# Chunk-selecting attention with a squared-ReLU layer behind it: the first three half-batches transposed on TensorE and placed from PSUM

## The chip, the cores and the metric

One core of a Trainium2 chip runs the whole program. The metric is the device time of one execution in microseconds (us). TensorE is called PE below, VectorE DVE, ScalarE ACT, GpSimd POOL and the SyncE queue SP, as in the rows of the profile.

## The reference

Four batches, eight heads, 768 positions, head width 64. The keys of a head are cut into 24 chunks of 32. For each query an upper bound of its score with each chunk is worked out from the chunk's smallest and largest key values, chunks that lie ahead of the query are ruled out, and the six best chunks are kept. Attention runs over the kept chunks under the causal mask, and a layer with a squared ReLU follows:

```
k_min, k_max = min and max of k over each chunk of 32
ub     = sum_d max(q * k_min, q * k_max)          # one bound per query and chunk
sel    = the 6 chunks with the largest ub, causal
scores = where(sel & causal, q k^T / 8, -1e9)
x      = softmax(scores) v                        # [3072, 512] over all heads
out    = relu(x w_in)^2 w_out                     # 512 -> 2048 -> 512
```

## The kernel before

**Slots.** A batch is cut into two halves of 384 queries (a *half-batch*, `hb` 0 to 7), and the eight heads into four pairs. One half-batch of one pair is a *slot*: `slots` (L171) counts 32 of them, four for each `hb`. The order of the work is written out by hand: nothing is reordered, each engine takes its instructions in program order, and waits are placed where one engine needs another's result.

**What a slot does.** `step_P` (L290) brings keys and queries of a pair into the transposed layout (width on partitions), takes minima and maxima of the key chunks (`extrema`, L184: two DVE reductions and a product into `kbd`) and the two ReLUs of the queries, `qr`. `step_U` (L298) multiplies them into the bounds `ub` on PE and finds the sixth largest with DVE's MAX8; the comparison is written beside the queries as a 0/1 row block. `step_V` (L320) transposes that block on PE and copies it out of PSUM into `qc`, so that one matmul of `kc` by `qc` in `step_E` (L347) gives score and penalty at once; ACT takes the exponential, and POOL cuts the diagonal blocks with an affine_select (L366). `step_F` (L374 to L395) multiplies by the values, and DVE divides (L391, L392). `kc` holds the keys in one half of the partitions and the chunk codes (`oneh`) in the other, and the two heads of a pair have them the other way round, so that one head's rows have to change partitions.

**Running ahead.** While slot s is in `step_E`, `step_U` and `step_V` are those of slot s+1, and `step_P` that of slot s+2.

**How keys and queries get there.** For `hb` 0 `stage` (L101) loads f32 by 16 DMAs on the SP and ACT queues; `step_cast` (L177) casts keys on DVE and queries on ACT, and `step_T0` (L195) transposes on PE into two PSUM tiles, `tk` for the keys and `tq` for the queries. For `hb` 1 `step_T1` (L250) transposes on PE, ACT copies both to SBUF (L260), and four small SP DMAs per slot (`place_k` L230, `place_q` L237) move them into `kc` and `qc`. From `hb` 2 on six DMA transposes per half-batch (`tr`, L265, on SP) write `kT` and `qT`, four larger SP DMAs place them, and `step_K` (L274) takes the extrema of all four pairs on DVE in two passes, for minima and maxima.

**The other work.** The layer behind the attention is cut into 16 `ffn_up` pieces (L432: four matmuls, ReLU on ACT or DVE, square on DVE) and 12 `ffn_down` pieces per half-batch, kept in `queue` and drawn by `fill` and `f1` between the attention steps. The ups of `hb` 0 run in the slots 4 to 8; the downs begin in slot 8. Loads from HBM other than the staged ones are casting DMAs on the POOL queue. `at(s, ...)` (L475) notes loads, chunk codes and DMA transposes for a slot, and `go` (L518) issues them there.

The PSUM pools are `psS` (three score tiles), `psF` (two, for `ph` and the transposes), `psY` (one, for the downs) and `psA` (two, tag `att`, for `ub`, `qt`, `po`, `pt`). Two lines set what the text below turns on, the DMA transposes of `hb` 2 and the place of the placing of slot 6, both on SP:

```
at(s0 + (i // 3 if hb > 2 else 0), tr, hb, "kq"[i // 3], i % 3)   # L514: all six of hb 2 in slot 4
(place_k if n == "k" else place_q)(1, p, p + 1)                   # L261: step_P(6) issues it at the end of slot 4
```

Of the kernel before, what the change touches and what calls it, by code (L numbers as in the profile page):

```python
# [14 lines left out]


CH = 32
TOPK = 6
HT = 3
# [5 lines left out]

# [4 lines left out]
)  # L30


@with_exitstack
def kernel(
# [30 lines left out]

    QROW = (D, 0)
    SROW = (0, D)
    kcs = [[consts.tile([128, NP, S], BF16, tag=f"kc{i}_{h}", name="kc") for h in range(2)]
           for i in range(2)]
    qcs = [consts.tile([128, NP, 2, HB], BF16, tag=f"qc{i}", name="qc") for i in range(2)]  # L70
# [3 lines left out]

# [13 lines left out]
    def load_v(b, h0, h1, j0, j1):  # L88
        if j1 - j0 == 1:
            nc.gpsimd.dma_start(  # L90
                out=vn[b % 2][:, h0:h1, j0, 0:D],
                in_=v[b, h0:h1, 128 * j0:128 * j1].rearrange("h p d -> p h d"))
        else:
            nc.gpsimd.dma_start(
                out=vn[b % 2][:, h0:h1, :, 0:D],
                in_=v[b, h0:h1].rearrange("h (j p) d -> p h j d", p=128))


    staged = []

    def stage(p, pool):  # L101
        t = []
        for eng, src in ((nc.sync, k), (nc.scalar if p < 2 else nc.sync, q)):
            x = pool.tile([128, HT, 2, D], F32, tag=f"st{len(t)}", bufs=NP, name="stage")
            for hh in range(2):
                eng.dma_start(
                    out=x[:, :, hh, :],
                    in_=src[0, 2 * p + hh, 0:HB].rearrange("(j p) d -> p j d", p=128))
            t.append(x)
        staged.append(t)  # L110

    ctx.enter_context(tc.manual_schedule())
    early = ExitStack()
    epool = early.enter_context(tc.tile_pool(name="early", bufs=NP))
    for p in range(NP):
        stage(p, epool)

    oneh = consts.tile([D, S], BF16, tag="oneh")
    nc.vector.memset(oneh, 0.0)
    cmask = consts.tile([128, HT, 2, NC], BF16, tag="cmask", name="cmask")  # L120
    nc.vector.memset(cmask, 0.0)
    ident = consts.tile([128, 128], BF16, tag="ident")
    make_identity(nc, ident)
    nc.gpsimd.affine_select(
        out=oneh, in_=oneh, compare_op=ALU.not_equal, fill=OFFSEL,
        base=0, channel_multiplier=1, pattern=[[-1, NC], [0, CH]])

    for g in range(4):
        nc.gpsimd.affine_select(
            out=cmask[g * 32:(g + 1) * 32], in_=cmask[g * 32:(g + 1) * 32],  # L130
            compare_op=ALU.is_ge, fill=NEG,
            base=12 + g, channel_multiplier=0,
            pattern=[[4, HT], [0, 2], [-1, NC]])
# [11 lines left out]
    for h in range(2):  # L145
        nc.vector.tensor_copy(
            kcs[0][h][SROW[h]:SROW[h] + D, :, 0:HB],
            oneh[:, 0:HB].unsqueeze(1).to_broadcast([D, NP, HB]))
# [3 lines left out]
    def codes(i, p, c0):  # L152
        for h in range(2):
            nc.vector.tensor_copy(kcs[i][h][SROW[h]:SROW[h] + D, p, c0:S], oneh[:, c0:S])

    def clear():
        nc.gpsimd.memset(vn[1][:, :, :, D:D + 1], 1.0)
        for i in range(3):
            nc.gpsimd.memset(nsel[i], 0.0)

# [13 lines left out]
    kbd = {}  # L174


    def step_cast(p):  # L177
        t = staged[p]
        kst = work.tile([128, HT, 2 * D], BF16, tag="kst", name="kst")
        nc.vector.tensor_copy(kst.rearrange("p j (h d) -> p j h d", h=2), t[0])  # L180
        nc.scalar.copy(qn0[:, :, p, 1:3, :], t[1])
        st[p] = {"kst": kst}

    def extrema(kt, s):  # L184

# [9 lines left out]
    def step_T0(s):  # L195

        p = s
        t = st[s]
        tk = psF.tile([128, HB], BF16, tag="ph", name="tk")
        tq = psF.tile([128, HB], BF16, tag="ph", name="tq")  # L200
        for j in range(HT):
            nc.tensor.matmul(tk[:, 128 * j:128 * (j + 1)], lhsT=t["kst"][:, j, :],
                             rhs=ident, is_transpose=True, start=True, stop=True)
        for j in range(HT):
            nc.tensor.matmul(tq[:, 128 * j:128 * (j + 1)],
                             lhsT=qn0[:, j, p, 1:3, :].rearrange("p h d -> p (h d)"),
                             rhs=ident, is_transpose=True, start=True, stop=True)
        qr = t["qr"] = work.tile([128, 2, HB], BF16, tag="qr", bufs=3, name="qr")
        nc.scalar.activation(qr[:, 0, :], tq, ACT.Relu, scale=-1.0)
        nc.scalar.activation(qr[:, 1, :], tq, ACT.Relu)  # L210
        extrema(tk, s)
        nc.vector.tensor_copy(kcs[0][0][D:128, p, 0:HB], tk[0:D])
        t["tk"] = tk

    def step_T0b(s):
        nc.scalar.copy(kcs[0][1][0:D, s, 0:HB], st[s]["tk"][D:128])
# [3 lines left out]
    def half_T(hb):  # L220
        if hb not in tT:
            tT[hb] = [work.tile([128, NP, HB], BF16, tag=f"{n}T", name=f"{n}T")
                      for n in "kq"]
        return tT[hb]

    def place_k(hb, p0, p1):
        kT = tT[hb][0]
        c = HB * (hb % 2)
        for h in range(2):
            nc.sync.dma_start(  # L230
                out=kcs[hb // 2 % 2][h][QROW[h]:QROW[h] + D, p0:p1, c:c + HB],
                in_=kT[D * h:D * h + D, p0:p1, :])

    def place_q(hb, p0, p1):
        qT = tT[hb][1]
        for h in range(2):
            nc.sync.dma_start(  # L237
                out=qcs[hb % 2][QROW[h]:QROW[h] + D, p0:p1, h, :],
                in_=qT[D * h:D * h + D, p0:p1, :])

    def relus(s):
        qT = tT[s // NP][1]
        t = st.setdefault(s, {})
        qr = t["qr"] = work.tile([128, 2, HB], BF16, tag="qr", bufs=3, name="qr")
        p = slots[s][2]
        nc.vector.tensor_scalar(qr[:, 0, :], qT[:, p, :], -1.0, 0.0,
                                op0=ALU.mult, op1=ALU.max)
        nc.vector.tensor_scalar_max(qr[:, 1, :], qT[:, p, :], 0.0)

    def step_T1(s):  # L250

        b, half, p = slots[s]
        for n, dst in zip("kq", half_T(1)):
            x = psF.tile([128, HB], BF16, tag="ph", name=f"t{n}")
            for j in range(HT):
                nc.tensor.matmul(
                    x[:, 128 * j:128 * (j + 1)],
                    lhsT=nat[n, b, HT + j][:, 128 * p:128 * (p + 1)],
                    rhs=ident, is_transpose=True, start=True, stop=True)
            nc.scalar.copy(dst[:, p, :], x)  # L260
            (place_k if n == "k" else place_q)(1, p, p + 1)  # L261
        extrema(tT[1][0][:, p, :], s)
        relus(s)

    def tr(hb, n, j):  # L265

        b, half = hb // 2, hb % 2
        nc.sync.dma_start_transpose(  # L268
            out=half_T(hb)["kq".index(n)][:, :, 128 * j:128 * (j + 1)],
            in_=nat.pop((n, b, HT * half + j)))  # L270

    kms = {}

    def step_K(hb, w):  # L274
# [3 lines left out]
        x = tT[hb][0].rearrange("p a (c j) -> p (a c) j", j=CH)  # L278
# [11 lines left out]
    def step_P(s):  # L290
        if s >= 2 * NP:
            relus(s)
        elif s >= NP:
            step_T1(s)
        else:
            step_T0(s)
# [353 lines left out]
```

## Time and profile before

| what | value |
|---|---|
| median of three runs | 306.75 us (306.55 to 307.5) |
| span of the profiled execution, first to last instruction | 305.8 us |
| that execution's own time | not listed apart from the runs; the median lies 0.95 us over the span |
| PE busy | 258.0 us (84%) |
| DVE, ACT busy | 174.4 us, 174.2 us (57% each) |
| POOL busy | 92.0 us (30%) |
| mean granted PE clock | 0.959 |

The page cuts the span into 40 slices of 7.6 us and writes the busy share of each engine in tenths. A row of the timeline has start, duration, engine, line, operation, output and inputs, and in brackets the idle time of the engine ahead of it with what ended it. A row of the waits has the waiting instruction, what it waited for, the sum, the number of times and the longest. A row of the windows has a stretch, its length, then busy time and instructions of PE, PE's weight load, DVE, ACT and POOL, the granted clock, the DMA share and GB/s.

### The profile page before, as it was taken

To read this page: it belongs to the slowest core of one execution; us is meant where nothing else is said; L and a number is where in the kernel's file an instruction comes from. 1 tells how busy PE (TensorE), PEld (TensorE's weight loads), DVE (VectorE), ACT (ScalarE), POOL (GpSimd) and SP (SyncE) were. 2 spreads that over 40 slices of the span, in tenths; PEclk is the share of its full clock that TensorE was granted. 3 is DMA by queue.
4 is the path that set the end of the run, shared out by engine and by line. 5 is a ranking of instruction groups with operands and counts; after the bars stand their busy time and mean duration, and the time that the engine had idled before them with its cause. 6 is when DMAs were issued, how large, how long until landed. Compare 5 with 4: busy or idle time off the path is not lost.

```text
span 305.8 us, 6296 instructions
## 1 busy us (share of the span) xinstructions
PE 258.0 (84%) x2260; PEld 157.7 (52%) x2260; DVE 174.4 (57%) x648; ACT 174.2 (57%) x372; POOL 92.0 (30%) x136
## 2 busy tenths in 40 slices
PE   2776682076589998999999989999999999999994
PEld 1554351054355655666556556665565666555541
DVE  6796684039777852775377537754775453332321
ACT  4584663036256684777666847776668677544300
POOL 8967441014434242353341423511112011000000
PEclk9999798579689999999999999999999999999999
DMA  9999999999957759799798398995442100010011
GB/s 159 158 187 111 176 124 179 157 162 146 130 41 59 146 81 146 72 177 166 95 143 160 66 147 85 168 143 102 89 139 71 51 12 26 34 38 34 35 70 69
DMA packets 117008, 33.32 MB, mean 109 GB/s; under 512 B 103664, under 2 KB 112880, under 8 KB 116976
## 3 DMA queue, kind: packets, MB, share of 16 engines
q0 software_dynamic: 71568, 12.85, 60.4%
q1 hardware_dynamic: 43808, 19.67, 31.4%
q10 hardware_dynamic: 1600, 0.39, 0.6%
q8 instruction: 18, 0.29, 0.5%
q14 instruction: 14, 0.11, 0.1%
HBM read 27.26 MB, written 6.29 MB: 110 GB/s over the span
## 4 chain that ended last, share of the span: by engine, by line
PE 64%; DMA 10%; SPq 9%; DVE 8%; ACT 5%; issue 2%; POOL 1%; POOLq 0%; DVEq 0%; ACTq 0%
PE py L454 24%; PE ph L435 21%; PE ps L357 9%; PE po L382 6%; SPq L268 6%; DMA qc<-qT 6%; DMA xT<-x 3%; SPq L419 2%; ACT e L362 2%; PE ub L307 1%; DVE kst L180 1%; ACT ht L442 1%; DVE km L282 1%; DMA stage<-in_k_dram 1%; ACT qc L344 1%
## 5 line engine op out<-in xcount | busy, mean ns | idle before, releaser
L362 ACT ACTIVATE e<-ps 128x512 bf16<-128x512 f32 x192 | 96.3, 549 | 40.1 <-PE ps L357 39.4
L435 PE MATMUL ph<-xT,w_in 128*128 128x384 bf16 x512 | 104.3, 331 | 7.3 <-ACT kT L260 3.3
L454 PE MATMUL py<-w_out,h 128*128 128x512 bf16 x384 | 96.6, 379 | 0.0
L444 DVE TENSOR_TENSOR h<-ht 128x384 bf16<-128x384 bf16 x128 | 47.8, 376 | 76.2 <-ACT ht L442 75.6
L442 ACT ACTIVATE ht<-ph 128x384 bf16<-128x384 f32 x120 | 58.9, 494 | 46.6 <-PE ph L435 44.7
L366 POOL TENSOR_SCALAR_AFFINE_SELECT e<-e 128x384 bf16<-128x384 bf16 x64 | 34.0, 532 | 167.6 <-ACT e L362 167.4
L357 PE MATMUL ps<-qc,kc 128*128 128x384 bf16 (+2 forms) x320 | 59.3, 291 | 16.0 <-DMA qc<-qT 14.3
L435 PEld LDWEIGHTS <-w_in 128*128 128x128 bf16 x512 | 47.7, 99 | 40.3 <-issue 8.5
L454 PEld LDWEIGHTS <-h 128*128 128x128 bf16 x384 | 35.8, 98 | 31.3
L357 PEld LDWEIGHTS <-kc 128*128 128x128 bf16 x320 | 28.1, 101 | 33.1 <-issue 17.2
L382 PEld LDWEIGHTS <-e 128*128 128x128 bf16 x672 | 27.3, 101 | 7.7 <-POOL e L366 2.7
L382 PE MATMUL po<-vn,e 128*128 128x65 bf16 x672 | 28.8, 198 | 2.1 <-POOL e L366 1.4
L314 DVE MAX8 m<-ub 128x8 f32<-128x24 f32 (+1 forms) x160 | 16.6, 169 | 6.3 <-PE ub L307 6.2
L83 POOL DMA_DIRECT2D qn<-in_q_dram x21 | 18.7, 901 | 0.1
L83 POOL DMA_DIRECT2D kn<-in_k_dram x21 | 18.6, 894 | 0.1
L392 DVE TENSOR_TENSOR x<-po,r 128x384 bf16<-128x384 f32 x32 | 17.8, 557 | 1.1
L460 ACT COPY ob<-py 128x512 f32<-128x512 f32 x18 | 10.7, 593 | 9.2 <-PE py L454 9.1
L282 DVE TENSOR_TENSOR km<-km 128x384 bf16<-128x384 bf16 (+3 forms) x48 | 13.8, 287 | 1.7
L338 PE MATMUL qt<-ident,nsel 128*128 128x128 bf16 x72 | 8.7, 222 | 6.4 <-DVE nsel L315 5.8
L440 DVE TENSOR_SCALAR ht<-ph 128x384 bf16<-128x384 f32 x8 | 4.4, 553 | 16.8 <-PE ph L435 16.6
L307 PE MATMUL ub<-kbd,qr 128*128 128x48 bf16 (+1 forms) x160 | 9.5, 180 | 4.9 <-DVE kbd L191 2.7
L343 DVE COPY qc<-qt 64x384 bf16<-64x384 bf16 (+1 forms) x28 | 8.9, 317 | 5.8 <-PE qt L338 5.8
(68 smaller groups left out, 166.5 us busy)
## 6 DMA issues: line engine op xcount, KB each, us to landing
out_dram<-ob SPq DMA_DIRECT2D x24, 256.0 KB, 2.2
kn<-in_k_dram POOLq DMA_DIRECT2D x21, 128.0 KB, 4.2
qn<-in_q_dram POOLq DMA_DIRECT2D x21, 128.0 KB, 5.3
vn<-in_v_dram POOLq DMA_DIRECT2D x6, 384.0 KB, 8.0
kc<-kT SPq DMA_DIRECT2D x12, 192.0 KB, 6.6
qc<-qT SPq DMA_DIRECT2D x12, 192.0 KB, 6.7
w_in<-in_moe_w_in_dram POOLq DMA_DIRECT2D x2, 1024.0 KB, 10.8
w_out<-in_moe_w_out_dram POOLq DMA_DIRECT2D x1, 2048.0 KB, 25.0
```

The source lines that it names most:

```text
L83: nc.gpsimd.dma_start(out=t.rearrange("p (h d) -> p h d", d=D), in_=(q if n == "q" else k)[b, :, 128 * j:128 * (j + 1)] .rearrange("h p d ...
L268: nc.sync.dma_start_transpose(out=half_T(hb)["kq".index(n)][:, :, 128 * j:128 * (j + 1)], in_=nat.pop((n, b, HT * half + j)))
L282: nc.vector.tensor_tensor(y, x[:, :, 0:m], x[:, :, m:2 * m], op=op)
L357: nc.tensor.matmul(ps[:, at:at + 128 * m], lhsT=kcs[b % 2][hh][:, p, 128 * j:128 * (j + 1)], rhs=qcs[half][:, p, hh, c:c + 128 * m], start ...
L362: nc.scalar.activation(e[:, 512 * n + lo:512 * n + hi], ps[:, lo:hi], ACT.Exp, scale=float(scale))
L366: nc.gpsimd.affine_select(out=d, in_=d, compare_op=ALU.is_ge, fill=0.0, base=0, channel_multiplier=-1, pattern=[[0, 3], [1, 128]])
L382: nc.tensor.matmul(po[:, hh, i, :], lhsT=t["e"][hh][:, c:c + 128], rhs=vn[b % 2][:, 2 * p + hh, j, :], start=(j == 0), stop=(j == iq))
L392: nc.vector.tensor_mul(x[:, :, 128 * p:128 * (p + 1)].rearrange("p j (h d) -> p h j d", h=2), po[:, :, :, 0:D], r.to_broadcast([128, 2, HT ...
L435: nc.tensor.matmul(ph[:, 0:HB], lhsT=w_in[:, ki, 128 * f:128 * (f + 1)], rhs=xT[:, ki, :], start=(ki == 0), stop=(ki == NKI - 1))
L442: nc.scalar.activation(ht, ph[:, 0:HB], ACT.Relu)
L444: nc.vector.tensor_mul(h, ht, ht)
L454: nc.tensor.matmul(py[t], lhsT=h2[hb, f][:, 128 * t:128 * (t + 1)], rhs=w_out[:, f, :], start=(f == 0), stop=(f == NFI - 1))
```

## The change

- `kc` and `qc` become one tile `kq` with four blocks of 384 columns per pair: keys and queries of the first half, keys and queries of the second.
- `hb` 0, 1 and 2 (`ON_PE = 3`) go through one `step_T`: keys and queries of a slot are transposed on PE into *one* PSUM tile `x`, ACT takes the two ReLUs from it, DVE the extrema, and `place` copies the rows from PSUM into `kq`, on DVE and, for the second head of `hb` 0, on ACT. No ACT copy, no DMA transpose and no placing DMA is left for these three. `step_K` is called for `hb` 3 on, both passes at pair 2.
- Of `hb` 0 only pair 0 is staged; the other three are loaded cast by six POOL DMAs, and `pack` copies their queries beside the selection block.
- `oneh` is worked out by one DVE product from the identity; the chunk codes are copied by DVE (first half of even batches), ACT (second half, noted for slot 1) and POOL (odd batches, slots 4 and 5).
- `w_in` is loaded in four pieces, two before slot 0 and two in slot 2; `w_out` in two pieces in slot 3; the loads of `hb` 1 move from ahead of slot 0 to slots 0 and 1, those of `hb` 2 from slot 3 to slot 4.
- From `hb` 3 on two placing DMAs per half-batch in place of four.
- Of the 16 ups of `hb` 0 a quarter has its ReLU on DVE, and not half; the fourth slot of `hb` 1 draws four.

```diff
-        tk = psF.tile([128, HB], BF16, tag="ph", name="tk")
-        tq = psF.tile([128, HB], BF16, tag="ph", name="tq")
...
-            nc.scalar.copy(dst[:, p, :], x)
-            (place_k if n == "k" else place_q)(1, p, p + 1)
...
+    def step_T(s, pool, tag):
+        b, half, p = slots[s]
+        t = st.setdefault(s, {})
+        x = pool.tile([128, 2, HB], BF16, tag=tag, name="tkq")
...
+        nc.scalar.activation(qr[:, 0, c:], x[:, 1, c:], ACT.Relu, scale=-1.0)
+        nc.scalar.activation(qr[:, 1, c:], x[:, 1, c:], ACT.Relu)
+        extrema(x[:, 0, :], s)
+        t["tkq"] = x
+        place(s, 0, nc.vector.tensor_copy)
+        if s >= NP:
+            place(s, 1, nc.vector.tensor_copy)
+    def pack(p):
+        nc.vector.tensor_copy(qn0[:, :, p, 1:3, :].rearrange("p j h d -> p j (h d)"),
+                              n0[1][:, :, p, :])
+    def place(s, h, copy):
+        b, half, p = slots[s]
+        x = st[s]["tkq"]
+        n = 1 if s < NP else 2
+        copy(kqs[b % 2][h][QROW[h]:QROW[h] + D, p, 2 * half:2 * half + n, :],
+             x[D * h:D * h + D, 0:n, :])
+    def place_dma(hb):
+        for h in range(2):
+            nc.sync.dma_start(
+                out=kqs[hb // 2 % 2][h][QROW[h]:QROW[h] + D, :, 2 * (hb % 2):2 * (hb % 2) + 2, :],
+                in_=half_T(hb)[D * h:D * h + D])
     def step_P(s):
+        hb = s // NP
+        if hb >= ON_PE:
             relus(s)
+        elif s < NP + 2:
+            step_T(s, psF, "ph")
+        elif s < 2 * NP + 2:
+            step_T(s, psY, "py")
         else:
+            step_T(s, psA, "att")
     def step_V(s, act=False):       # for s < NP
-            nc.vector.tensor_copy(qc[:, p], qt)
+            nc.vector.tensor_copy(qc(s, 0), qt[:, 0])
+            nc.scalar.copy(qc(s, 1), qt[:, 1])
-        if hb == 0 and f % 2:       # which ups have their ReLU on DVE
+        if hb == 0 and f % 4 == 3:
+    def codes(i, half, copy):
         for h in range(2):
+            copy(kqs[i][h][SROW[h]:SROW[h] + D, :, 2 * half, :],
+                 oneh[:, HB * half:HB * half + HB].unsqueeze(1).to_broadcast([D, NP, HB]))
+    for g in range(2):
+        at(-1, load_w_in, 512 * g, 512 * g + 512)
+    at(-1, load_v, 0, 4, 8)
     at(0, clear)
+    for i, x in enumerate(load_half(1)):
+        at(i // 3, *x)
+    for g in range(2, 4):
+        at(2, load_w_in, 512 * g, 512 * g + 512)
+    for g in range(2):
+        at(3, load_w_out, 8 * g, 8 * g + 8)
+    at(1, codes, 0, 1, nc.scalar.copy)
+    at(4, codes, 1, 0, nc.gpsimd.tensor_copy)
+    at(5, codes, 1, 1, nc.gpsimd.tensor_copy)
     for x in load_half(2):
-        at(3, *x)
+        at(4, *x)
-    for hb in range(2, 2 * B):
+    for hb in range(ON_PE, 2 * B):
         s0 = 4 * hb - 4
         for i in range(2 * HT):
-            at(s0 + (i // 3 if hb > 2 else 0), tr, hb, "kq"[i // 3], i % 3)
-        at(s0 + 2, place_k, hb, 0, NP)
-        at(s0 + 2, place_q, hb, 0, NP)
+            at(s0 + i // 3, tr, hb, "kq"[i // 3], i % 3)
+        at(s0 + 2, place_dma, hb)
-    step_cast(0)
+    step_cast()
+    go(-1, 99)
     step_P(0)
-    step_T0b(0)
-    step_cast(1)
-    go(-1, 99)
+    nc.vector.tensor_scalar_mul(
+        oneh.rearrange("p (c j) -> p c j", j=CH),
+        ident[0:D, 0:NC].unsqueeze(2).to_broadcast([D, NC, CH]), OFFSEL)
+    place(0, 1, nc.scalar.copy)
     step_U(0)
+    codes(0, 0, nc.vector.tensor_copy)
     step_V(0)
     step_P(1)
-    step_cast(2)
-        if s + 1 < NP: step_T0b(s + 1)       # in the loop over slots 0 to 3
         if s + 1 < NP:
-            step_T0b(s + 1)
+            place(s + 1, 1, nc.scalar.copy)
+            pack(s + 1)
...
-        if hb < 2 * B - 1:
-            if p == 1 and hb > 1 or p == 2 and hb == 1:
+        if ON_PE - 1 <= hb < 2 * B - 1:
+            if p == 2:
                 step_K(hb + 1, 0)
-            if p == 2:
                 step_K(hb + 1, 1)
-            if p == 1 and hb > 1 or p == 2 and hb == 1: step_K(hb + 1, 0)
-            if p == 2: step_K(hb + 1, 1)
+            if p == 2: step_K(hb + 1, 0); step_K(hb + 1, 1)      # from hb 2 on
```

208 lines of the change are left out of this document (76 added, 132 removed).

## The prediction

> **What bounds the kernel now.** The page first: its span, PE's busy share by slice, and the DMA engines'.
>
> ```profile
> span 305.8 us, 6296 instructions
> PE   2776682076589998999999989999999999999994
> DMA  9999999999957759799798398995442100010011
> ```
>
> PE is full from the twelfth slice on and thin before. One stretch of the windows (length, then busy time of PE, its weight load, DVE, ACT, POOL, granted clock) and the waits of PE before 82 us name the hole:
>
> ```profile
> 50.00:60.00 10.00, 0.00 (x0) 0.00 (x0) 0.00 (x0) 0.00 (x0) 0.00 (x0) 0.60 1.36 175
> PE ps L357 <- DMA qc<-qT: 14.3, 1, 14.3
> PE ph L435 <- ACT kT L260: 3.3, 3, 1.3
> ```
>
> Between 50 and 60 us no engine computes. With PE full later on, a gain has to come from the first 81 us. The timeline of SP says why:
>
> ```profile
> 38.92 13.01 SPq L268 DMA_TRANSPOSE qT<-qn  x3
> 53.31 1.19 SPq L237 DMA_DIRECT2D qc<-qT  x2
> 63.02 1.01 PE L357 MATMUL ps<-qc,kc 128*128 128x384 bf16 x4 [14.28 <-DMA qc<-qT]
> 81.11 1.49 PE L435 MATMUL ph<-xT,w_in 128*128 128x384 bf16 x4
> ```
>
> SP is busy with the transposes of `hb` 2 until 51.9 us (38.92 + 13.01), although slot 8 needs them only after 80 us. The placing of slot 6, whose data was ready, is issued behind them at 53.31 and waited for until 63.02. Slot 6 could have begun at 48.7 (63.02 - 14.28). The row at 81.11 is the last up of `hb` 0, at the start of slot 8.
>
> **What goes.** With `hb` 1 and 2 placed by DVE from PSUM, SP has nothing to do until the transposes of `hb` 3. The 14.3 us go for certain; the question is what the new path costs. I follow it to the start of slot 8, with windows cut at the first score matmul of a slot as the base (slots 0, 2, 3, 4 and 5).
>
> ```profile
> 9.37:13.69 4.32, 3.24 (x24) 2.23 (x24) 3.38 (x12) 3.39 (x8) 4.26 (x7) 1.00 2.20 154
> 19.50:23.09 3.59, 3.00 (x35) 2.25 (x35) 3.29 (x13) 3.46 (x9) 3.04 (x5) 1.00 1.29 201
> 23.09:33.48 10.39, 6.30 (x67) 3.72 (x66) 6.63 (x26) 4.65 (x10) 7.21 (x10) 0.90 1.84 121
> 33.48:41.13 7.65, 5.32 (x42) 3.34 (x43) 5.56 (x19) 5.27 (x11) 2.16 (x3) 0.91 1.30 192
> 41.13:48.30 7.17, 5.97 (x77) 4.24 (x75) 6.61 (x24) 5.54 (x12) 3.87 (x4) 1.00 1.41 104
> ```
>
> **A wait that the change adds: one PSUM tile for two engines.** The trace of before shows that ACT and DVE never read one PSUM tile together. L343 (DVE) and L344 (ACT) read different partitions of `qt` and write different places:
>
> ```profile
> L344 ACT COPY qc<-qt x13: 367/367/474, 30.7 to 229.6; 64x256 bf16<-64x256 bf16 x9, 64x384 bf16<-64x384 bf16 x4
>   DVE qc L343: 5.2, 9
> ```
>
> Nine times of 13 ACT stood idle until DVE's copy was done. Before, `tk` and `tq` were two tiles, so DVE's reductions ran beside ACT's ReLUs. `step_T` has one tile: extrema now stand behind both ReLUs, and these behind the second `qc` copy. Queued behind the waiting reduction are `kbd`, the place, MAX8, the divisions and the next `qc`; PE's `ub` and `qt` wait for those.
>
> The Trainium skill (PSUM — Partial Sum Buffer, section PSUM bank collisions raise a hardware error) says that two engines must not touch the same bank in the same 32-partition quadrant at once, reads included, while different quadrants are safe. The trace is stricter, since L344 waits for a reader of other quadrants; ReLUs and reductions share all quadrants, so by the rule too the order stays, and the rival in which it is free gets a smaller chance.
>
> **Start and slots 0 to 2,** on the rows of the start and of one undisturbed slot:
>
> ```profile
> 5.37 0.56 DVE L189 TENSOR_REDUCE km<-tk 128x12 bf16<-128x384 bf16 x1 [0.60 <-PE tk L202]
> 6.34 0.49 ACT L210 ACTIVATE qr<-tq 128x384 bf16<-128x384 bf16 x1
> 7.03 0.36 DVE L180 CAST kst<-stage 128x384 bf16<-128x384 f32 x1
> ```
>
> ```profile
> 19.36 0.55 DVE L189 TENSOR_REDUCE km<-tk 128x12 bf16<-128x384 bf16 x1
> 20.41 0.18 DVE L191 TENSOR_TENSOR kbd<-hmask,km 128x48 bf16<-128x48 bf16 x1
> 20.62 0.35 DVE L212 COPY kc<-tk 64x384 bf16<-64x384 bf16 x1
> 21.00 0.41 DVE L314 MAX8 m<-ub 128x8 f32<-128x12 f32 x4
> 21.71 0.51 PE L328 MATMUL qt<-ident,qn 128*128 128x128 bf16 x6
> 21.79 0.20 DVE L391 RECIPROCAL r<-po 128x6 f32<-128x6 f32 x1
> 22.02 0.56 DVE L392 TENSOR_TENSOR x<-po,r 128x384 bf16<-128x384 f32 x1
> 22.50 0.55 DVE L333 COPY qc<-qt 128x768 bf16<-128x768 bf16 x1
> ```
>
> *Start:* the first reduction moves from 5.37 to the end of the ReLU, 6.34 + 0.49, so 1.5 us later. `oneh` (64x768, its input repeated) and the codes come between, for which these rows stand, with two ACT copies for the slope:
>
> ```profile
> L146 DVE COPY kc<-oneh x2: 601/613/625, 2.6 to 3.2; 64x1536 bf16<-64x1536 bf16 x2
> 1.39 0.99 POOL L124 TENSOR_SCALAR_AFFINE_SELECT oneh<-oneh 64x768 bf16<-64x768 bf16 x1
> 22.52 0.47 ACT L260 COPY kT<-tk 128x384 bf16<-128x384 bf16 x1
> 28.14 0.80 ACT L414 COPY xT<-pt 128x768 bf16<-128x768 bf16 x1 [2.66 <-PE pt L409]
> ```
>
> `oneh` lies between 0.3 (half an L146) and 1.0 us (POOL's time for the same tile); I take 0.85, near POOL's row, as the repeated input is unlike a plain copy. The kernel before had the cast at 7.03 in that place, so +0.5. Two code copies (1.2) lie beside `qt` (0.75, with its waits), +0.45; a `qc` copy of half the width (0.35 for 0.55), -0.2. First score matmul: 9.37 + 2.25 = 11.6.
>
> *One slot, counted from the end of the first `qc` copy:* ACT's `qc` copy to 0.5; ReLUs to 1.4; reductions to 2.4; `kbd` to 2.6; place to 3.0; MAX8 and comparison to 3.7; `pack` (an estimate of 0.25) to 3.95. PE does `po` (24 matmuls, 1.0 us) from 3.1, so `qt` runs to 4.6, DVE's divisions to 4.9, and the next `qc` copy ends at 5.25. The undisturbed slot took 3.59, so +1.65. Slot 0 has no `po`: 4.9. Slot 1: 5.25. In slot 2 ACT has the codes of `hb` 1 ahead of its exponentials: two copies of 64x1536, each 0.47 + 3 x 0.33 = 1.46 by the slope, 2.9 in all (between 1.2, two L146, and 4). Standing ahead of the exponentials they delay the last score matmul and `po`; with ACT's 3.46 of work in a slot of 5.25 I let 0.8 be hidden, so +2.1: 7.35. Slot 3 then starts at 11.6 + 4.9 + 5.25 + 7.35 = 29.1, 6.0 late. The loads should keep up: 768 packets each for `load_0`, less than the `kn` tiles before, and fewer staged bytes ahead of them.
>
> **Slots 3 to 7** go by these rows as well:
>
> ```profile
> 30.03 0.36 DVE L444 TENSOR_TENSOR h<-ht 128x384 bf16<-128x384 bf16 x1 [2.03 <-ACT ht L442]
> 30.31 0.34 DVE L343 COPY qc<-qt 64x384 bf16<-64x384 bf16 x1
> 44.83 0.63 DVE L314 MAX8 m<-ub 128x8 f32<-128x24 f32 x6
> 45.49 0.31 DVE L315 TENSOR_TENSOR nsel<-ub,m 128x144 bf16<-128x144 f32 x1
> ```
>
> Slot 3 loses 1.9 (ReLUs before reductions, two places where two short ReLUs stood) and gains 2.8: `qc` was there at 30.65 (30.31 + 0.34), but the score matmul of slot 4 came at 33.48, behind ACT's `kT` copies, the reductions and the codes; the codes are there already now. 10.39 - 0.9 = 9.5, slot 4 at 38.6.
>
> ACT had 5.54 us of work in slot 5 and gets one more ReLU of an up (0.49), two ReLUs standing where two copies stood: 6.0. DVE's round is extrema (1.0), `kbd` (0.2), two places (1.1, the 0.55 row each), reciprocal and division (0.75), three squares (1.05), MAX8 and comparison (1.0), then `qt` on PE (0.35) and the first `qc` (0.35): 5.8. Two exponentials and the ReLUs on ACT close it with 1.7: 7.5 a slot, beside 7.65 and 7.17 before, and 8.5 for slot 4, which starts a phase early. PE no longer waits for `kT` (the 3.3 us of the waits), as `psY` holds the tiles; this is in the 7.5. Slot 8 starts at 38.6 + 8.5 + 3 x 7.5 - 0.65 (its first up stands ahead of the score) = 69.0, where 81.1 stood: **-12.1**.
>
> **POOL copies.** What stands with them in POOL's order:
>
> ```profile
> L83 POOL DMA_DIRECT2D kn<-in_k_dram x21 | 18.6, 894 | 0.1
> L94 POOL DMA_DIRECT2D vn<-in_v_dram x2 | 2.8, 1420 | 0.3 <-issue 0.3
> ```
>
> Slots 4 and 5 get two copies of 64x1536 each: twice the 0.99 row for a copy, so 4.0 a slot (bounds 1.2, two L146, and 8). POOL had 5.5 and 3.3 us to spare in these slots (7.65 - 2.16, 7.17 - 3.87). Behind copies and loads stand the affine_selects, on which `po` waits. With six loads of 0.9 moved into slot 4, and the values' loads of 1.4 in slot 5, the second select of slot 5 comes about 1 us after PE wants it: **+1.0** (0 to 5). The Trainium skill (GPSIMD Engine Reference, section Elementwise — side-by-side cycle accounting) gives 1.8 cycles an element at 1.2 GHz at best, an estimate of 2.3 us a copy. By that the term would be 1.6; no run here shows a POOL copy yet.
>
> **From slot 8 on**, PE sets the pace.
>
> ```profile
> 81.10:111.00 29.90, 27.92 (x250) 17.53 (x249) 21.27 (x83) 18.16 (x41) 8.95 (x14) 0.92 0.75 87
> 71.90 1.35 DVE L282 TENSOR_TENSOR km<-km 128x384 bf16<-128x384 bf16 x4
> ```
>
> Twelve transposes for slots 10 and 11 are new on PE, twice the 0.51 row of six: **+1.0**. The clock of 0.92 here follows the idle stretches; at 1.0 some of 30 x 0.08 = 2.4 us come back, and I take **-1.0**, as slot 8's start still idles. Both `step_K` passes (four of five products of one in the row above, 2 us in all) fall in one slot: **+0.5** (0 to 2.5); ups and downs on PE cover the rest. Two placing DMAs fewer on SP: nothing, SP has room after 81 us.
>
> **Sum:** 305.8 - 12.1 + 1.0 + 1.0 - 1.0 + 0.5 = 295.2. The median of the runs lies 0.95 above the span: 296.15, **296.0 us** for short.
>
> **Rivals.** *(a) The order within the tile is no bound:* DVE and ACT find other work, the start comes 1.5 us earlier than in the forecast, and so do slots 0 to 2 each: 296 - 6 = 290. For it: DVE is idle a fifth of such a slot; against it: every step of the round is on the path. *(b) The wait moves to POOL or to the loads:* `hb` 2's tiles, loaded in slot 4 behind `w_out`, or the selects behind copies of 4 us: the upper bound of that term, +4 to +6: 301. For it: the DMA row stands at 9 for eleven slices. *(c) Slower:* in slots 4 to 7 ACT and DVE take turns in place of overlapping: ReLUs come last in ACT's queue, and the next exponentials wait for the DVE round. A slot is then ACT's 6.0 and the round without the squares, 4.75: 10.75 in place of 7.5, four times 3.25, 296 + 13 = 309. It decides from 2.7 us a slot (10.75 in all). Against it: before, too, the reductions of these slots came behind an ACT copy, in slots of 7.2. That the stall doesn't go is no rival, since no DMA is left on slot 6's path.
>
> **How the numbers follow.** Forecast 0.52, (a) 0.19, (b) 0.17, (c) 0.12. Faster holds the first three but for a tail of (b): 0.85; within 0.3%, about what a measurement of this kernel can tell from no change, 0.04; slower 0.11. The range leaves out (c) and the far tails: 285 (rival (a) with the low bounds of `oneh` and codes, 3 to 5 us) to 304 (rival (b) with the high bounds of POOL).
>
> **What would show it.** No gap over 3 us in PE between 40 and 60 us; reductions that start when the second ReLU ends; first scores at 11.6 and slot 4 at 38.6; slot 8 near 69 to 70; ACT copies of 1.46; POOL copies near 2.0. I am wrong if slots 0 to 2 take under 4 us, if a slot of `hb` 1 takes over 9, or if PE waits for POOL for more than 3 us.

## The result and the profile after

The changed kernel is **slower**: 319.25 us median of five runs (317.27 to 323.59) against 307.5 (306.55 to 309.56) for the kernel before in the same session, a ratio of 1.0366 (95% interval 1.0294 to 1.0437). The ratios leave out the executions that the record marks as slow, here the one of 323.59 us. Forecast were 296.0 us and a range of 285 to 304.

Span and PE by slices on the page of the changed kernel:

```profile
span 317.6 us, 6256 instructions
...
PE   0147584978598796989997989989979999999994
```

The hole of before in the seventh and eighth slices (PE at 2 and 0) is gone. In its place PE does nothing in the first slice and little in the second, and the later slices have more 7s and 8s. For a ledger the span is cut at three events that both kernels have: the values of slot 7 (`po`, the last of the attention of `hb` 1), the first DMA transpose of the attention's output (of `hb` 2, at the start of slot 12), and the first DMA of the last such group (of `hb` 6). Windows of before, then of after (length, busy time of PE, its weight load, DVE, ACT and POOL, granted clock):

```profile
0.00:82.39 82.39, 44.49 (x433) 29.55 (x434) 52.86 (x183) 39.34 (x84) 40.79 (x61) 0.88 1.59 154
82.39:110.72 28.33, 26.35 (x241) 16.71 (x240) 20.74 (x80) 17.12 (x38) 8.80 (x13) 0.93 0.70 85
110.72:233.48 122.76, 118.78 (x1082) 72.76 (x1081) 74.64 (x304) 83.85 (x181) 38.25 (x54) 1.00 1.01 123
233.48:305.80 72.32, 68.38 (x509) 38.72 (x507) 26.21 (x81) 33.85 (x71) 4.17 (x8) 0.99 0.13 43
```

```profile
0.00:79.50 79.50, 45.85 (x445) 32.66 (x446) 48.74 (x167) 43.12 (x92) 47.41 (x66) 0.96 1.27 117
79.50:113.85 34.35, 27.32 (x255) 16.93 (x253) 24.06 (x86) 19.51 (x46) 10.71 (x15) 0.95 0.78 82
113.85:245.18 131.33, 119.97 (x1082) 72.95 (x1081) 74.48 (x304) 84.01 (x181) 38.20 (x54) 1.00 1.00 115
245.18:317.60 72.42, 68.38 (x509) 38.70 (x507) 26.23 (x81) 33.88 (x71) 4.18 (x8) 0.99 0.13 43
```

The first stretch is 2.9 us shorter where 12.1 were forecast. The second is 6.0 longer, the third 8.6 longer at the same clock and with the same instructions, the last the same: -2.9 + 6.0 + 8.6 + 0.1 = 11.8, the difference of the spans. So there are two separate questions: what ate 9 us at the start, and what ails every half-batch from `hb` 2 on. The waits of PE in after name a candidate for each:

```profile
PE tkq L193 <- DVE kn L177: 14.0, 1, 14.0
PE ub L280 <- DVE qr L235: 7.5, 5, 1.7
```

**The start.** Before, PE waited 4.8 us for the first cast keys; now 14.0. DVE's timeline and POOL's, in after:

```profile
2.57 0.38 DVE L131 MEMSET qn<- 128x384 uint32 x1
13.35 0.60 DVE L177 CAST kn<-stage 128x384 bf16<-128x384 f32 x1 [10.41 <-issue]
13.47 0.10 DVE L132 MEMSET vn<- 128x48 bf16 x1
```

```profile
6.53 1.46 POOL L96 DMA_DIRECT2D vn<-in_v_dram  x1
```

DVE starts nothing between 2.95 and 13.35 us. The bracket says "issue", so no waited-for result is shown, but the program order says what was next: the `memset` of the ones column of `vn` (recorded beside the cast, though it stands ahead of it). In the changed kernel the first load of the values into the same tile is written above that `memset`:

```
    load_v(0, 0, 4)                                     # DMA into vn[0], columns 0 to 63 of each head
    ...
    nc.vector.memset(vn[0][:, :, :, D:D + 1], 1.0)      # L132: column 64 of each head
```

The columns differ, but they interleave in one tile, and the memset waits for the DMA. The trace gives 6.7 us from the issue of this load to its landing: 6.53 + 6.7 = 13.2. The cast behind it had its data long before (in kernel a below it starts at 4.41).

**The steady part.** Both passes of `step_K` are now called at pair 2. DVE in slot 14 of after, then PE:

```profile
138.09 0.56 DVE L252 TENSOR_TENSOR km<-kqT 128x768 bf16<-128x768 bf16 x1
138.68 1.14 DVE L252 TENSOR_TENSOR km<-km 128x384 bf16<-128x384 bf16 x4
...
142.02 0.28 DVE L256 TENSOR_TENSOR kbd<-km,hmask 128x48 bf16<-128x48 bf16 x2
142.21 0.22 DVE L235 TENSOR_SCALAR qr<-kqT 128x256 bf16<-128x256 bf16 x1
```

```profile
142.49 0.37 PE L280 MATMUL ub<-kbd,qr 128*128 128x24 bf16 x4 [1.12 <-DVE qr L235]
```

4.1 us of DVE in one block (138.09 to 142.21), with the ReLUs of the next slot's queries queued behind it, and PE's bounds behind those.

### The profile page after: what moved, and what is told of

It reads as the page before. It is cut to its first block, busy times and chain, and to the rows that moved or that the text cites. A ratio compares the mean times of both kernels' runs of the same rounds, so it can differ in the third digit from the quotient of the medians.

```text
span 317.6 us, 6256 instructions
## 1 busy us (share of the span) xinstructions
PE 261.5 (82%) x2284; PEld 161.2 (51%) x2284; DVE 173.5 (55%) x637; ACT 180.5 (57%) x387; POOL 100.5 (32%) x142
## 4 chain that ended last, share of the span: by engine, by line
PE 56%; DVE 19%; ACT 9%; issue 7%; DMA 6%; SPq 1%; POOL 1%; ACTq 0%; POOLq 0%; DVEq 0%
PE py L430 21%; PE ph L411 19%; PE ps L334 7%; DVE km L252 5%; PE po L359 4%; DMA xT<-x 4%; ACT e L339 3%; DMA w_in<-in_moe_w_in_dram 2%; DVE kq L213 2%; DVE h L420 2%; SPq L395 1%; DVE km L170 1%; PE ub L280 1%; ACT ht L418 1%; DVE km L171 1%
## 5 line engine op out<-in xcount | busy, mean ns | idle before, releaser
L420 DVE TENSOR_TENSOR h<-ht 128x384 bf16<-128x384 bf16 x128 | 50.8, 401 | 82.5 <-ACT ht L418 82.3
L418 ACT ACTIVATE ht<-ph 128x384 bf16<-128x384 f32 x124 | 61.1, 496 | 53.6 <-PE ph L411 51.8
L334 PE MATMUL ps<-kq 128*128 128x384 bf16 (+2 forms) x320 | 60.2, 294 | 2.1 <-ACT e L339 1.9
L334 PEld LDWEIGHTS <-kq 128*128 128x128 bf16 x320 | 28.4, 102 | 16.7 <-issue 1.6
L84 POOL DMA_DIRECT2D qn<-in_q_dram x21 | 18.6, 891 | 0.0
L193 PE MATMUL tkq<-ident,kn 128*128 128x128 bf16 x36 | 5.5, 281 | 14.0 <-DVE kn L177 14.0
L280 PEld LDWEIGHTS <-qr 128*128 128x128 bf16 x160 | 7.9, 99 | 17.0 <-DVE qr L235 8.7
L170 DVE TENSOR_REDUCE km<-tkq 128x12 bf16<-128x384 bf16 x12 | 6.7, 557 | 14.1 <-ACT qr L198 13.4
```

The costliest lines, as they stand in the source:

```text
L84: nc.gpsimd.dma_start(out=t.rearrange("p (h d) -> p h d", d=D), in_=(q if n == "q" else k)[b, :, 128 * j:128 * (j + 1)] .rearrange("h p d ...
L280: nc.tensor.matmul(ub[:, j - j0], lhsT=st[s]["qr"][:, w, 128 * j:128 * (j + 1)], rhs=kbds[b % 2][:, p, w, :, 0:ncs], start=False, stop=(j ...
L334: nc.tensor.matmul(ps[:, at:at + 128 * m], lhsT=kqs[b % 2][hh][:, p, 2 * (j // HT), 128 * (j % HT):128 * (j % HT + 1)], rhs=qc(s, hh)[:, c ...
L418: nc.scalar.activation(ht, ph[:, 0:HB], ACT.Relu)
L420: nc.vector.tensor_mul(h, ht, ht)
```

## The experiments

Theory: two accidents of order, the memset behind a load and the two passes in one slot, cost 9 us and 8 us; without them the forecast's path holds. Rival: the start is limited by the loads, and the new round (one PSUM tile, places on DVE) is too long everywhere, so that little comes back. The first kernel undoes one, the second the other, the third both.

**a: the load behind the memset** (after, one line moved).

```diff
-    load_v(0, 0, 4)          # above the masks
...
     nc.vector.memset(vn[0][:, :, :, D:D + 1], 1.0)
+    load_v(0, 0, 4)
```

> The changed kernel with one line moved: the first load of values is issued after DVE has written the column of ones into the same tile, and not before. Theory 1 (the memset of the ones waits for that load, and the cast of the staged keys stands behind it on DVE): the cast moves from 13.35 us to about 4.4, the first score matmul from 19.8 to 11.6, the time from 319 to 311. Rival (the staged keys come late because nine casting loads share the DMA engines): the cast stays near 13, the time near 319.

Measured: 309.84 us (307.41 to 316.06), 9.4 less than after; ratio to before 1.0029 (0.9997 to 1.0061). Its profiled execution was the longest of them (316.06 us), so only DVE's first rows are read:

```profile
3.07 0.10 DVE L131 MEMSET vn<- 128x48 bf16 x1
4.41 0.55 DVE L177 CAST kn<-stage 128x384 bf16<-128x384 f32 x1 [1.25 <-DMA stage<-in_k_dram]
```

The memset runs at once, and the cast waits for its own data alone. The one line is worth about 9 us.

**b: the two key passes in two pairs** (after).

```diff
-            if p == 2:
+            if p == 1:
                 step_K(hb + 1, 0)
+            if p == 2:
                 step_K(hb + 1, 1)
```

> The changed kernel with step_K as it was: minima at pair 1, maxima at pair 2. Theory 2 (both passes in one slot make the next bounds wait for DVE): PE's wait of 7.5 us for the ReLUs behind step_K goes, each half-batch from 3 to 6 is 1.5 to 2 us shorter, the time falls from 319 to 310 to 312. Rival (from slot 8 on the kernel is slower by its two placing DMAs per half-batch or by the later xT transposes): the half-batches stay at 36 and 30 us and the time within 1.5 us of 319.

Measured: 310.78 us (307.07 to 313.63), 8.5 less than after; ratio 1.0055 (1.0017 to 1.0093). The waits for `qr` are gone, and the third stretch of the ledger is 123.27 us long:

```profile
112.72:235.99 123.27, 117.89 (x1066) 72.80 (x1081) 74.00 (x304) 83.97 (x181) 38.14 (x54) 1.00 1.06 123
```

8.1 us of the 8.6 came from this call: 2.0 us a half-batch on average, in four of them.

**c: both.**

> The changed kernel with both edits: the memset ahead of the load, and step_K in two slots. If the two costs lie one behind the other and add up: 319 - 8 - 8 = 303, so 4 us under the kernel before. If the later part is a floor that absorbs the earlier start (loads that arrive no sooner): 308 to 311.

Measured: **299.68 us** (298.45 to 301.75), ratio 0.9729 (0.9681 to 0.9777): faster than before. The two edits together give 19.6 us, alone 9.4 and 8.5; the 303 expected had 8 for each. The ledger of c:

```profile
0.00:70.27 70.27, 46.15 (x445) 32.94 (x446) 48.68 (x167) 43.11 (x92) 47.77 (x66) 0.95 1.44 131
70.27:102.81 32.54, 26.84 (x252) 16.74 (x253) 23.97 (x86) 19.53 (x46) 10.35 (x15) 0.95 1.08 88
102.81:226.12 123.31, 117.88 (x1066) 72.78 (x1081) 74.06 (x304) 83.97 (x181) 38.06 (x54) 1.00 1.10 123
226.12:298.50 72.38, 67.97 (x501) 38.68 (x507) 26.21 (x81) 33.86 (x71) 4.16 (x8) 0.99 0.13 43
```

The first stretch is 12.1 us shorter than before, the third 0.55 longer, the last equal. What still lacks is the second, +4.2 us: the slots of `hb` 2 themselves. The theory holds, and the rival is right about those slots only.

**d: the kernel before, placing of `hb` 1 on POOL's queue**, to get it out from behind SP's transposes.

```diff
-            nc.sync.dma_start(
+            (nc.gpsimd if hb == 1 else nc.sync).dma_start(     # in place_k and place_q
```

> The kernel before with one part of the change's effect alone: the placing DMAs of half-batch 1 go out on POOL's queue, past the DMA transposes on SP. Theory of the prediction (the 14.3 us are the order on SP): the wait of slot 6 falls from 14.3 to under 3 us and the time from 307 to 294 to 297. Rival (the DMA engines are full then, and the placing would land no sooner): a wait of over 8 us stays, the time is 301 or more.

Measured: 314.71 us (311.48 to 316.69), ratio 1.0175 (1.0105 to 1.0244). PE still waits 13.2 us for `qc`, yet this doesn't speak against SP's order, since the placing now stood still on POOL:

```profile
52.32 0.55 POOL L230 DMA_DIRECT2D kc<-kT  x1 [3.60 <-DMA w_in<-in_moe_w_in_dram]
65.70 0.55 POOL L230 DMA_DIRECT2D kc<-kT  x1 [12.83 <-DMA w_out<-in_moe_w_out_dram]
```

POOL's next DMA was not issued before the weights had landed. The experiment only moved the wait to another queue and told nothing; **h** asks the question again.

**h: the kernel before, transposes of `hb` 2 issued two slots later**, behind slot 7's placing. One constant:

```diff
-            at(s0 + (i // 3 if hb > 2 else 0), tr, hb, "kq"[i // 3], i % 3)
+            at(s0 + (i // 3 if hb > 2 else 2), tr, hb, "kq"[i // 3], i % 3)
```

> The kernel before with one line changed: the DMA transposes of half-batch 2 are issued in slot 6 in place of slot 4, behind the placing of slot 7's queries. Theory, that SP's order alone makes the wait of 14.3 us: the wait of the score matmul of slot 6 for its queries falls under 3 us, some of it comes back where the keys of half-batch 2 are due (slot 6 and 7), and the time is 293 to 300 us. Rival, that the DMA engines are full and the placing would land late anyway: a wait over 8 us stays and the time is over 301 us.

Measured: 299.23 us (297.99 to 300.95), ratio 0.9749 (0.969 to 0.9808). The wait for `qc` fell from 14.3 to 0.8 us, so **SP's order made it**: the queries of slot 6 are placed by a DMA issued at 40.63 us in place of 53.31, and it lands after 5.8 us in place of 9.7. So they lie ready 16.5 us earlier: 12.7 by the place in the queue, 3.9 by the landing, which in before had transposes of `hb` 2 in flight beside it. Half of the wait comes back as a wait for the keys of `hb` 2, on which DVE's key passes and behind them `qr` wait (timelines of PE and of DVE in h):

```profile
66.11 0.42 PE L307 MATMUL ub<-kbd,qr 128*128 128x24 bf16 x4 [7.76 <-DVE qr L246]
```

```profile
61.21 0.56 DVE L282 TENSOR_TENSOR km<-kT 128x768 bf16<-128x768 bf16 x1 [6.57 <-DMA kT<-kn]
```

One constant gives what the whole change gives after mending (c): the intervals overlap for most of their length.

**i: the kernel before, `hb` 2 alone on the new path.** `step_T` of the change, written for the old tiles, for slots 8 to 11; no DMA transpose and no `step_K` for `hb` 2.

```diff
-        if s >= 2 * NP:
+        if s >= 3 * NP:
             relus(s)
+        elif s >= 2 * NP + 2:
+            step_T2(s, psA, "att")     # transposes, ReLUs, extrema, four places from one PSUM tile
+        elif s >= 2 * NP:
+            step_T2(s, psY, "py")
...
```

> The kernel before, with half-batch 2 alone on the new path: six transposes a slot on TensorE into one PSUM tile, ReLUs on ACT, extrema and four places on DVE from PSUM. Start, slots 0 to 5, tiles, codes and loads stay as they were. Theory, that of the three half-batches only this one pays, since it takes half-batch 2's transposes off SP's queue and its keys off the DMA engines: slots 0 to 6 as with the later issue of the transposes (slot 7 at 53), no wait of 7.8 us for the keys in slot 7, slot 8 near 61 in place of 70.7, and 288 to 291 us. Rival, that what is won before slot 8 is handed back behind it (weights, the ups' queue, TensorE's own work): the time stays at 296 us or above.

Measured: **297.62 us** (295.45 to 300.0), ratio 0.9629 (0.958 to 0.9679), below h's interval. The direction was right, but the time is 7 to 10 us over what was expected and lies where the rival had it (296 us or above): much of what is won before slot 8 is handed back behind it. Ledgers of h, then of i, with one stretch more:

```profile
0.00:72.77 72.77, 43.50 (x434) 29.05 (x434) 50.76 (x183) 39.30 (x84) 40.78 (x61) 0.86 1.65 170
72.77:101.15 28.38, 26.29 (x241) 16.68 (x240) 20.84 (x80) 17.12 (x38) 8.75 (x13) 0.94 0.87 96
101.15:134.81 33.66, 32.28 (x322) 20.48 (x321) 20.23 (x80) 23.80 (x51) 13.98 (x18) 1.00 1.39 135
```

```profile
0.00:64.42 64.42, 43.62 (x446) 29.89 (x447) 49.98 (x172) 39.84 (x87) 40.20 (x61) 0.95 1.64 164
64.42:98.46 34.04, 27.54 (x250) 17.11 (x252) 26.63 (x97) 19.64 (x45) 9.44 (x14) 0.90 0.81 86
98.46:135.51 37.05, 33.57 (x317) 21.48 (x321) 20.13 (x80) 23.93 (x51) 13.84 (x18) 0.95 1.48 122
```

8.35 us are won up to the values of slot 7. 5.7 go in `hb` 2's own slots, where DVE has 5.8 us more to do. PE waits 3.6 us there for the division of slot 7, which stands in DVE's order behind the extrema and places of slot 9, and 1.8 us where `ub` waits for a place copy. Another 3.4 go in the next half-batch, in this execution: PE waited 3.2 us there for a DMA transpose of the output, at a clock of 0.95. Whether that last part belongs to the edit or to that execution stays open; that the same wait is 1.8 us in j, which has the same path for `hb` 2, and 1.2 in c speaks for the execution.

**j: `hb` 1 as well.** As i, with `step_T2` from slot 4 on.

> As the one before it, with half-batch 1 on the same path too (12 more matmul transposes replaced in kind, no SP placing left before half-batch 3). Theory, that the round through one PSUM tile is longer than ACT's copies with placing by DMA: slots 4 to 7 took 31.3 us in the version with copies on POOL and 29.9 with codes on DVE, against some 28.5 here, so 1 to 3 us slower than with half-batch 2 alone: 289 to 294 us. Rival, that fewer ACT copies and no placing DMA make these slots shorter: the same time or up to 2 us less.

Measured: 301.42 us (300.1 to 303.19), ratio 0.9773 (0.973 to 0.9817), 3.8 us slower than i, where 1 to 3 were expected; the intervals are apart. The values of slot 7 begin at 69.47 against 64.42. `hb` 1 was transposed on PE already; what the edit adds is the one tile and the places on DVE, and here they cost rather than gain, once the SP queue is free. More than half of the 5 us falls in slot 3 (13.80 us against 11.12): PE's score matmul waits 3.7 us in place of 1.0 for the chunk codes, since DVE's copies of them (L154) now stand behind the extrema and four places of slot 5. That part is the place of the code copy in DVE's order; whether it would go with the copy moved was not tried.

**g: c with `hb` 2 by DMA again** (`ON_PE = 2`).

> Same base, with only the first two half-batches on TensorE; half-batch 2 is loaded, transposed and placed by DMA as in the kernel before. Theory, that the first up-front wait of slot 6 came from half-batch 1's placing standing behind half-batch 2's transposes: with half-batch 1 placed from PSUM there is no PE wait over 3 us between 40 and 60 us, and the time is 297 to 301 us (1 us of transposes less on PE, the step for the keys of the next half without a PSUM tile held). Rival, that the 16 DMA engines are too full for half-batch 2's transposes: a wait of 4 us or more for its keys before slot 8, and 304 us or more.

Measured: 301.19 us (298.55 to 302.45), ratio 0.9798 (0.9724 to 0.9872), not to be told from c. No wait for `hb` 2's keys appeared before slot 8; the rival falls. The time is 0.2 us over the range that was expected. The only PE wait over 3 us between 40 and 60 us is one of 3.4 us for DVE's comparison, the same as in c. Placing `hb` 1 without SP is enough to end the stall.

**e: c with two PSUM tiles**, to price the order within one tile.

```diff
-        x = pool.tile([128, 2, HB], BF16, tag=tag, name="tkq")
+            x = [pool.tile([128, HB], BF16, tag=tag, name="tkq") for _ in range(2)]   # slots 0 to 3
...
```

> Base: the version with the ones ahead of the load and the two key passes in two pairs (299.68 us, first score matmul at 10.65, slots 0 to 2 of 5.0, 4.9 and 7.0 us). Here the transposed keys and queries of slots 0 to 3 lie in two PSUM tiles again. Theory, that the order between ACT's ReLUs and DVE's reductions in one tile is on the path of every round: the reduction starts about 1 us earlier at the start (first score matmul near 9.6), and slots 0 to 2 are shorter by 1 to 1.6 us each, so 295 us or a little less. Rival, that the round is bound by ACT's and DVE's own work and the order only moves idle time: slots 0 to 2 change by less than 0.3 us each and the time stays at 299 to 300 us.

Measured: 302.73 us (300.18 to 303.58), ratio 0.9835 (0.9755 to 0.9916). Windows of slots 0, 1 and 2, cut at the first score matmuls:

```profile
10.47:14.32 3.85, 3.05 (x23) 2.20 (x23) 2.80 (x12) 3.16 (x9) 1.74 (x5) 1.00 1.60 186
14.32:18.07 3.75, 3.65 (x38) 3.08 (x37) 3.37 (x14) 3.17 (x9) 3.69 (x8) 1.00 1.63 190
18.07:26.52 8.45, 3.96 (x38) 2.81 (x37) 3.30 (x13) 6.53 (x11) 7.22 (x11) 0.74 1.95 121
```

In c these slots took 5.01, 4.89 and 6.97. The order in the tile is worth 1.15 us a slot in slots 0 and 1, as the theory has it. The start gains 0.2 us and not 1: the first reduction comes 1.0 us earlier, but `oneh` behind it takes 1.38 us in place of 0.55. Slot 2 gives 1.5 back at once: PE waits 3.1 us for ACT's exponentials, behind the code copies, and 1.2 us for the loads of `hb` 1. The largest loss comes in slot 5, of 11.56 us against 8.21 in c. Two of DVE's squares stand beside POOL's code copies there, and PE waits 4.1 us for the comparison behind them, 0.8 in c. Rows of DVE, POOL and PE in e:

```profile
49.35 3.43 DVE L424 TENSOR_TENSOR h<-ht 128x384 bf16<-128x384 bf16 x2
49.56 3.01 POOL L141 COPY kq<-oneh 64x1536 bf16<-64x1536 bf16 x2
54.80 0.50 PE L320 MATMUL qt<-ident,nsel 128*128 128x128 bf16 x3 [4.07 <-DVE nsel L292]
```

The time of e is over the theory's 295 and over the rival's 299 to 300; the rival's mechanism, slots that hardly change, is not what happened.

**f: c with the codes of batch 1 on DVE.**

```diff
-    at(4, codes, 1, 0, nc.gpsimd.tensor_copy)
-    at(5, codes, 1, 1, nc.gpsimd.tensor_copy)
+    at(4, codes, 1, 0, nc.vector.tensor_copy)
+    at(5, codes, 1, 1, nc.vector.tensor_copy)
```

> Same base (slots 3 and 4 of 10.7 and 10.4 us, beside which POOL copies 64x1536 twice in 3.12 us). Here DVE makes these four copies, in the same slots. Theory, that POOL's copies stretch DVE's work on SBUF (squares of 1.4 us and more in place of 0.36) and so lengthen the round: the squares beside them go back to under 0.5 us, DVE pays 1.2 us a slot for the copies, and the two slots together get 2 to 3 us shorter: 297 to 298 us. Rival, that the round of DVE is full and 1.2 us a slot more cost what they are: 300 to 302 us.

Measured: 300.02 us (298.35 to 301.17), ratio 0.9767 (0.9708 to 0.9826): by the time, nothing. By the profile the mechanism is there, smaller than expected: slots 4 and 5 together take 17.4 us in place of 18.6, where 2 to 3 us were expected. DVE and POOL in slots 4 and 5 of after, where POOL copies; then DVE in slot 4 of f:

```profile
50.83 2.94 DVE L420 TENSOR_TENSOR h<-ht 128x384 bf16<-128x384 bf16 x2
60.77 1.29 DVE L420 TENSOR_TENSOR h<-ht 128x384 bf16<-128x384 bf16 x1 [0.25 <-ACT ht L418]
62.80 0.80 DVE L420 TENSOR_TENSOR h<-ht 128x384 bf16<-128x384 bf16 x1
```

```profile
50.45 3.12 POOL L141 COPY kq<-oneh 64x1536 bf16<-64x1536 bf16 x2
60.27 3.12 POOL L141 COPY kq<-oneh 64x1536 bf16<-64x1536 bf16 x2
```

```profile
41.04 0.61 DVE L420 TENSOR_TENSOR h<-ht 128x384 bf16<-128x384 bf16 x2
41.58 1.12 DVE L141 COPY kq<-oneh 64x1536 bf16<-64x1536 bf16 x2
```

A square of 0.36 us takes up to 1.6 beside a POOL copy, and each ends just after one: for the second of the pair and the two of slot 5, 50.83 + 2.94 = 53.77 against 53.57, 62.06 against 61.83, 63.60 against 63.39. DVE does the four copies of a pair of slots in 2.2 us, POOL in 6.2 while holding DVE up for 2.2 us in slot 4 and 1.4 in slot 5 (the rows above less 0.36 for each square).

**k: e and f together.**

> The mended change (ones ahead of the load, key passes in two pairs) with two PSUM tiles for half-batch 0 and the codes of batch 1 on DVE: the two edits together that were tried apart. Theory, that the 3.4 us won in slots 0 and 1 by two tiles came back because half-batch 1's queries landed late and POOL's copies stretched the next slots: with the copies gone 1 us of it stays, 297 to 299 us. Rival, that nothing stays: 300 us or more.

Measured: **297.93 us** (297.42 to 298.21), ratio 0.966 (0.9614 to 0.9705), 4.8 us below e, with intervals apart, where the same edit gave nothing on c. The slots beside the code copies show why: 4 and 5 together take 20.9 us in e and 16.3 here, 18.6 in c and 17.4 in f. POOL's copies cost 4.5 us with two tiles and 1.2 with one, so their price hangs on what they meet. It is the best form of the whole change found here, and level with i.

**l: k with slot 9's transposes, extrema and places behind the division of slot 7.**

```diff
             step_X(hb - 1, hb == 2)
+            if hb == 2:
+                step_P(s + 1)
...
-        if s + 2 < NS:
+        if s + 2 < NS and s != 2 * NP - 1:
             step_P(s + 2)
```

> The version with two tiles and the codes on DVE (297.93 us), with the transposes, ReLUs, extrema and places of slot 9 issued in slot 8 behind the division of slot 7 and the transposes of its output, in place of ahead of them. Theory, that the wait of 2.9 us of TensorE for the divided output at the start of slot 8 is DVE's order (2.4 us of extrema and places stood ahead of the division): that wait falls under 0.6 us and 1.5 to 2.5 us are won: 295.5 to 296.5 us. Rival, that slot 9's bounds come late instead: TensorE waits for the bounds of slot 9 by 2 us or more and the time stays within 0.7 us of 298.

Measured: 301.61 us (299.71 to 303.41), ratio 0.9817 (0.9766 to 0.9869), slower than k. Waits of PE from 67 to 75 us in k, then in l:

```profile
PE pt L389 <- DVE x L373: 2.9, 1, 2.9
PE qt L320 <- DVE nsel L292: 0.3, 1, 0.3
```

```profile
PE ub L284 <- DVE kbd L172: 2.2, 1, 2.2
PE qt L320 <- DVE nsel L292: 1.1, 1, 1.1
PE pt L389 <- DVE x L373: 0.5, 1, 0.5
```

The wait for the division fell as it should, and the bounds of slot 9 came late in its place: 3.2 us of waits before, 3.8 after. The rival holds for the mechanism: DVE's work there is on the path in either order. The time is not equal, though, but 3.7 us longer. 2.4 of that shows in the profiled executions, and 2.1 of these in the stretch from the values of slot 7 to the output's first DMA transpose (k, then l):

```profile
67.26:100.25 32.99, 26.71 (x252) 16.82 (x253) 24.29 (x86) 19.43 (x46) 10.45 (x15) 0.95 0.80 86
66.78:101.82 35.04, 28.47 (x257) 17.84 (x258) 24.70 (x86) 20.14 (x46) 10.64 (x16) 0.90 0.86 82
```

PE's waits there are nearly alike (6.3 and 6.6 us); its own work takes 1.8 us more, at a granted clock of 0.90 in place of 0.95: the clock stands at 0.50 for 6.8 us in l (from 72.6) and for 3.4 in k (from 71.6). What keeps it low longer in this order was not tried.

## Why the prediction was wrong, point by point

- **The start (failed).** The sum had 11.6 us for the first score matmul, from four terms on DVE's and ACT's rows. In after it stands at 19.81. The order of DVE's setup against the new `load_v` was not looked at: the sum counts DVE's casts, reductions and copies, and takes nothing for its memset of the tile that the moved load fills. Kernel a: 9.4 us. Without the accident the terms were good, about 1 us too high: 10.65 in c, with `oneh` at 0.55 where 0.85 was taken.
- **Both `step_K` passes in one slot, +0.5 (0 to 2.5) (mis-sized).** Twice wrong. The quoted row holds four of the five products of one pass, and the text made 2 us of both passes; they are 4.1 us. And it was priced once, where it comes once for each half-batch: 2.0 us on average in each of the four half-batches of the third stretch, 8.1 us in all, and 1.8 in the stretch ahead of it (34.35 against 32.54 in c). "Ups and downs on PE cover the rest" failed since the next bounds are queued behind the block on DVE. These two points are 19.6 of the 23 us between forecast and result (319.25 - 296.0).
- **The stall goes, worth 12.1 us up to slot 8 (right in its cause, the number partly by luck).** In c the stretch up to the values of slot 7 is 82.39 - 70.27 = 12.1 us shorter. Counted at the last up of `hb` 0, the forecast's own mark, it is 13.7 (81.11 against 67.38, where that up comes before slot 8 starts), at the first scores of slot 8 10.6 (85.75 against 75.14). SP's order as its cause, read from the timeline, is shown by h. "No gap over 3 us in PE between 40 and 60 us" held but for one wait of 3.4 us in slot 4, for a comparison behind the squares that POOL's copies stretched.
- **One PSUM tile for two engines (right).** Each reduction starts at the end of the second ReLU; DVE waited in after 13.4 us in 11 places for ACT (`km` L170 behind `qr` L198). Kernel e puts it at 1.15 us a slot where 1.65 was taken for the whole lengthening.
- **Slots 0 to 2 of 4.9, 5.25 and 7.35 (right):** 5.01, 4.89 and 6.97 in c, with ACT code copies of 1.48 where 1.46 was expected.
- **Slots 3 to 6 of 9.5, 8.5, 7.5 and 7.5 (low by 3.7 us):** 10.74, 10.37, 8.21 and 7.34 in c, of which the second is over the 9 us for a slot of `hb` 1 that the prediction named as a sign against itself. Windows of slots 3 and 4 of c:

```profile
27.52:38.26 10.74, 7.98 (x67) 5.71 (x68) 5.94 (x19) 4.36 (x10) 4.00 (x6) 1.00 1.05 155
38.26:48.63 10.37, 6.21 (x45) 3.84 (x43) 7.71 (x19) 6.52 (x15) 7.78 (x9) 0.81 1.29 170
```

  Slot 4 has POOL at 7.8 us of work and DVE at 7.7, 2.9 of it two stretched squares, at a granted clock of 0.81. What slot 7 won (the values of slot 7 came 6.1 us after its first scores) and the earlier start (slot 3 at 27.52, forecast 29.1) made up for it; that errors of 4 us cancel in the 12.1 is luck.
- **POOL copies, "+1.0" on the selects (wrong mechanism).** They took 1.56 us each (2.0 by the row, 2.3 by the estimate from the Trainium skill's figure), the selects were hardly late (PE waits for POOL: 1.1 us in all in c), and the cost fell on DVE's squares. The Trainium skill has the rule (SBUF — State Buffer, section SBUF: two separate sides): a DVE operation with two SBUF inputs and a GpSimd operation that reads SBUF take a shared port pair in turn, each for its whole length. The rows agree to 0.2 us, and the division of slot 4's output, which reads PSUM, kept its 0.56 in the middle of a POOL copy. The prediction looked for POOL's cost on POOL alone.
- **From slot 8 on, +1.0 for the transposes and -1.0 for the clock (failed for `hb` 2's slots).** c is 4.2 us longer there: PE waits 2.9 us for the division behind slot 9's extrema and places, and 1.7 us where `ub` waits for a place copy out of a tile that takes its turn in `psA`. The forecast followed the new round through `hb` 1 and priced `hb` 2's at PE's transposes alone.
- **Rivals.** (b) named 301 for other reasons than the ones that gave 299.7 in c; (c), the only slower one, put the loss in slots 4 to 7, where c lost 1.9 in slot 4 and little behind. Neither accident was among them.

## What to carry to other kernels

When a load is moved up, look for every other writer of its tile, however small: a memset behind it holds its engine until the DMA lands, with all that is queued there. When work on an in-order engine is merged into one block, price it as a block, count how often it comes, and ask who is queued behind it. And ahead of a rebuilt path, try the smallest edit of the queue that causes the wait: one constant gave here what the whole rebuilding gave once its two accidents were mended (c); k, with two edits more, lies 1.3 us below it, with intervals that still touch.

## What the runs showed of the hardware

- A POOL copy of 64x1536 bf16 takes 1.56 us (DVE 0.56, ACT 1.48) and stretches DVE's SBUF-to-SBUF products beside it from 0.36 to 1.6 us in after and c (two in 3.43 us in e), but not the division that reads PSUM.
- A DMA of POOL's queue whose tile depends on nothing of the weights was issued only after the weight load ahead of it had landed, up to 12.8 us later (d). What makes it wait was not tried.
- The same DVE product `oneh` took 0.55 us in c and 1.38 in e, where it ran 1 us earlier, beside the issue of the values' load; the cause was not tried.
